# Three small waits of a matmul-bound kernel: phase ends moved to slot ends, one block's copies moved to VectorE, two more PSUM buffers for the last block

## The chip, the cores and the metric

One core of a Trainium2 chip runs the kernel. The metric is the device time in microseconds (us), as a median over runs of one execution each. The profile is one execution; its span is the time from the first to the last instruction, about 1.75 us less than the device time of the same run. TensorE is "PE" in the profile (its weight loads "PEld"), VectorE "DVE", ScalarE "ACT", GpSimd "POOL", SyncE "SP".

## The reference, cut to what matters

```python
# x: (8, 4096, 192) f32; weight: (8, 7): a causal convolution over 7 positions, one set of taps per head
w = softmax(weight, axis=-1)
y[b, s, d] = sum(w[d // 24, k] * x_padded[b, s + k, d] for k in range(7))
# moe_w_in: (192, 2048), moe_w_out: (2048, 192)
h = y.reshape(32768, 192) @ moe_w_in
out = (0.5 * h * (1 + erf(h / sqrt(2)))) @ moe_w_out     # exact GELU
```

## The kernel before

The 32768 tokens are worked on as two halves side by side: the two row halves of TensorE take one token half each. Each half is cut into 35 blocks: six of 256 tokens (0 to 5) and 29 of 512 (6 to 34). A block passes four engines:

- VectorE transposes x and does the convolution (`xT`, `acc`, `xc`). Blocks 0 and 1 are convolved on TensorE.
- TensorE multiplies with `win` into one of two PSUM buffers `hp` (each two banks). This is one *slot*; a block has 8 or 16.
- ScalarE takes the GELU of `hp` into `gT`. Slot u needs the buffer that GELU u - 2 has left.
- TensorE multiplies `gT` with `wout` into the four banks `ob`. This work is cut into *units*, and a share of the units of block n - 1 is issued behind the inner matmuls of each slot of block n.

The two groups of a 256-token block (128 tokens of each half) have two *phases* of 16 units each. In the second the row halves swap banks, and the program makes it wait for the first (`S_PH`; 0.29 us of load idle in the kernel before where nothing lies between them). The four groups of the last block are done after everything else.

```python
share = {1: [4, 8, 8, 8, 9, 9, 9, 9]}          # units of block 0 in the slots of block 1; blocks 2 to 5: 8 each

def mm2(m, g, ph, i):                          # one unit: two matmuls
    bb = banks(m, g)
    if i == 0:
        if ph == 0:
            wait_banks(t, m, g)
        else:
            t.wait_ge(S_PH, PHC[m] + g + 1)    # the first phase has ended
    if g == 0 and ph == 0:
        c = NCH[m]                             # units that one GELU serves: 2, or 1 in a 512-token block
        if i % max(c, 8) == 0:                 # GELUs of the next eight units
            last = min(NF, i + max(c, 8))
            t.wait_ge(S_GELU, SL0[m] + last // c)
    ...

def wait_banks(t, m, g):
    ...
    else:                                      # the last block
        e = k - G0[M1]                         # its group
        t.wait_ge(S_EV, EVC[M1] + (-2 if e == 0 else e - 1))   # group 1: all transposes of block 33
        if e >= 2:
            t.wait_ge(S_EVB, e - 1)

def evac(e, m, g):                             # blocks 0 to 5, on ScalarE
    ...
    e.activation(out=dst, in_=src, func=AF.Copy).then_inc(S_EVA)

m = NB - 1                                     # the last block's units
for g2 in range(0, NG[m], 2):
    for ph in range(2):
        for g in range(2):
            for i in range(NF):
                mm2(m, g2 + g, ph, i)
```

The first matmul of a block waits for VectorE's convolution of that block (`S_CV`) and for the GELU two slots back. VectorE's work on block 2 begins when x of block 2 has landed (at 19.65 us in the trace of the kernel before). SyncE issues the loads in the order x of blocks 0 and 1, the four quarters of `w_out`, x of block 2.

## Time and profile before

| | before |
|---|---|
| time, median of the 3 runs known at first | 683.61 us (683.43 to 683.99) |
| span of the profiled run | 681.6 us |
| PE busy | 675.0 us, 99% |
| DVE busy | 561.0 us, 82% |
| ACT busy | 537.3 us, 79% |

The order of reading is: busy shares on the page, busy time by stage, then the timeline at the few places where PE isn't full. PE's busy time can hold a wait (in the prediction's lines the 16 matmuls at 21.02 show 1.06 us against 0.82 for the next 16, with 0.29 us of load idle among them), so the *starts* of a slot's first weight load are the better ruler: each loss shows as a step. The prediction shows the lines.

### The profile page before, as it was taken

What the parts mean: (1) busy time and instruction counts of PE and PEld (TensorE: products, weight loads), DVE (VectorE), ACT (ScalarE), POOL (GpSimd) and SP (SyncE); (2) the same over time, 40 slices, a digit from 0 to 9 for tenths busy, and PEclk for the clock granted to TensorE, in tenths of its full rate; (3) what the DMA queues carried; (4) which work ended last, traced back from release to release, by engine and by line L of the source; (5) the groups of instructions that cost most, each with busy time, mean ns of one, the idle gap of its engine ahead of it and who ended that gap; (6) DMA issues with size and microseconds to landing.
All of it is one profiled execution on the core that took longest, in us unless ns stands there. A gap on an engine that the chain in (4) does not pass through costs nothing.

```text
span 681.6 us, 27317 instructions
## 1 busy us (share of the span) xinstructions
PE 675.0 (99%) x12576; PEld 410.1 (60%) x12576; DVE 561.0 (82%) x904; ACT 537.3 (79%) x550; POOL 38.9 (6%) x57
## 2 busy tenths in 40 slices
PE   8999999999999999999999999999999999999998
PEld 4899655555555555555555555555555555555556
DVE  6899979888889888899888898888898888988611
ACT  6899988787787777787777788777878777878772
POOL 5026000000000000000000000000000000000000
PEclk9999999999999999999999999999999999999999
DMA  9446323234332244332244422334322434310123
GB/s 222 86 101 134 79 60 75 43 75 95 96 94 58 45 91 94 95 86 47 60 94 95 94 69 46 78 94 96 94 52 46 95 94 96 83 42 21 48 49 94
DMA packets 132994, 54.79 MB, mean 80 GB/s; under 512 B 126480, under 2 KB 132752, under 8 KB 132880
## 3 DMA queue, kind: packets, MB, share of 16 engines
q1 hardware_dynamic: 130960, 51.50, 32.5%
q8 instruction: 98, 1.61, 1.0%
q0 software_dynamic: 1248, 0.79, 0.9%
q10 hardware_dynamic: 672, 0.76, 0.4%
q14 instruction: 16, 0.13, 0.1%
HBM read 28.66 MB, written 25.17 MB: 79 GB/s over the span
## 4 chain that ended last, share of the span: by engine, by line
PE 96%; ACT 2%; DMA 1%; issue 0%; DVE 0%; SPq 0%; ACTq 0%
PE hp L760 48%; PE ob L824 43%; PE ob L791 6%; ACT gT L681 2%; DMA xin<-in_x_dram 1%; PE ob L711 0%; ACT xc L191 0%; ACT osb L269 0%; DVE osb L311 0%; DVE xT L526 0%; ACT xTb L630 0%; SPq L872 0%; DVE osb L280 0%; SPq L329 0%; ACTq L629 0%
## 5 line engine op out<-in xcount | busy, mean ns | idle before, releaser
L681 ACT ACTIVATE gT<-hp 128x1024 bf16<-128x1024 f32 x512 | 523.3, 1024 | 128.8 <-PE hp L760 125.5
L760 PE MATMUL hp<-xc,win 64*64 64x512 bf16 (+2 forms) x6048 | 419.5, 366 | 1.5 <-ACT gT L681 0.7
L824 PE MATMUL ob<-gT,wout 64*64 64x512 bf16 x5376 | 366.3, 376 | 0.0
L559 DVE SCALAR_TENSOR_TENSOR acc<-xT,wcol,acc 128x512 f32<-128x512 f32 (+1 forms) x495 | 314.1, 698 | 0.0
L760 PEld LDWEIGHTS hp<-xc,win 64*64 64x64 bf16 (+1 forms) x6048 | 189.9, 106 | 134.8 <-ACT gT L681 2.5
L824 PEld LDWEIGHTS ob<-gT,wout 64*64 64x64 bf16 x5376 | 172.3, 118 | 122.8
L311 DVE STREAM_TRANSPOSE osb<-ob 128x512 f32<-128x512 f32 x84 | 74.1, 885 | 100.8 <-PE ob L824 100.8
L526 DVE STREAM_TRANSPOSE xT<-xin 128x512 f32<-128x512 f32 (+1 forms) x105 | 78.6, 797 | 3.8 <-DMA xin<-in_x_dram 3.8
L559 DVE SCALAR_TENSOR_TENSOR xc<-xT,wcol,acc 128x512 bf16<-128x512 f32 (+1 forms) x99 | 65.0, 708 | 0.0
L447 POOL COPY xT<-xT 128x18 f32<-128x18 f32 x30 | 27.9, 930 | 505.2 <-DVE xT L526 482.9
L791 PE MATMUL ob<-wout,gT 64*128 64x192 bf16 x1024 | 52.9, 243 | 0.3
L791 PEld LDWEIGHTS ob<-wout,gT 64*128 64x128 bf16 x1024 | 44.9, 94 | 5.2 <-PE ob L791 0.6
L552 DVE TENSOR_SCALAR acc<-xT,wcol 128x512 f32<-128x512 f32 (+1 forms) x90 | 37.5, 474 | 1.1
L282 ACT ACTIVATE osb<-ob 128x192 f32<-128x192 f32 x4 | 1.3, 332 | 9.5 <-PE ob L791 9.5
L280 DVE COPY osb<-ob 128x192 f32<-128x192 f32 x4 | 1.4, 358 | 8.4 <-PE ob L791 8.4
L695 PE MATMUL hp<-warm 128*128 128x512 bf16 x16 | 5.1, 485 | 1.3 <-DVE warm L463 1.3
L269 ACT ACTIVATE osb<-ob 128x384 f32<-128x384 f32 x12 | 5.8, 486 | 0.0
L654 ACT ACTIVATE acc<-xT,wcol 128x256 f32<-128x256 f32 (+1 forms) x9 | 5.2, 575 | 0.0
L695 PEld LDWEIGHTS hp<-warm 128*128 128x128 bf16 x16 | 1.8, 119 | 4.0 <-issue 1.9
L384 POOL DMA_DIRECT2D win<-in_moe_w_in_dram x6 | 3.9, 658 | 0.8 <-POOLq L905 0.8
L711 PE MATMUL ob<-xTb,dg 64*64 64x256 bf16 (+1 forms) x112 | 3.2, 245 | 0.7 <-ACT xTb L630 0.7
L193 DVE CAST xc<-ob 64x256 bf16<-64x256 f32 (+3 forms) x8 | 2.8, 357 | 1.3 <-PE ob L711 1.1
(31 smaller groups left out, 22.4 us busy)
## 6 DMA issues: line engine op xcount, KB each, us to landing
out_dram<-osb SPq DMA_DIRECT2D x122, 192.0 KB, 3.1
xin<-in_x_dram SPq DMA_DIRECT2D x116, 192.0 KB, 4.1
xin<-in_x_dram SPq DMA_DIRECT2D x20, 96.0 KB, 4.2
woutf<-in_moe_w_out_dram SPq DMA_DIRECT2D x4, 384.0 KB, 6.2
win<-in_moe_w_in_dram POOLq DMA_DIRECT2D x4, 96.0 KB, 4.6
win<-in_moe_w_in_dram POOLq DMA_DIRECT2D x2, 192.0 KB, 5.1
out_dram<-osb SPq DMA_DIRECT2D x8, 48.0 KB, 1.9
out_dram<-osb ACTq DMA_DIRECT2D x4, 96.0 KB, 1.9
```

The lines of the kernel that those rows point to most:

```text
L269: e.activation(out=dst, in_=src, func=AF.Copy).then_inc(S_EVA)
L311: v.transpose(ap(osb[m % 2], j, [[8 * C, 128], [C // 2, TB // 32], [NP, 32]]), bank(ring(m, j)),).then_inc(S_EV)
L447: g.tensor_copy(dst, src).then_inc(S_HALO)
L526: v.transpose(ap(xT[n % 2], p * XW + HX, [[NP * XW, 128], [1, w]]), ap(xin[n % NX], p, [[TB // 32 * DQ, 128], [D if n == 0 else DQ, w // 3 ...
L552: ins = v.tensor_scalar(a, src, wk, None, ALU.mult)
L559: ins = v.scalar_tensor_tensor(dst, src, wk, a, op0=ALU.mult, op1=ALU.add)
L654: a.activation(out=acc[n % 2][:, p * TB : p * TB + w], in_=ap(xT[n % 2], p * XW + HX, [[NP * XW, 128], [1, w]]), func=AF.Copy, scale=wcol[ ...
L681: a.activation(out=ap(gT[n % 2], i * c * 2 * w, dst), in_=ap(hp[u % 2], 0, src), func=AF.Gelu,).then_inc(S_GELU)
L695: t.matmul(hp[1][:, 0:512], warm[:, 0:128], warm[:, :])
L760: ins = t.matmul(hp[u % 2][fo : fo + fw, o : o + w], ap(win, f1, [[NP * F, 64], [2, fw]]), xc[n % 2][r, p * TB : p * TB + w], start=(p == ...
L791: ins = t.matmul(bank(bb[sub], w=C), gT[m % 2][r, c0 : c0 + 128], wout[r, CH[sub][i] * C : (CH[sub][i] + 1) * C], start=(ph == 0 and i == ...
L824: ins = t.matmul(bank(ring(m, j), slice(64 * h, 64 * h + 64), w), ap(wout, 64 * hf * NF * C + CH[h][i] * C + j, [[NF * C, 64], [NP, 64]],) ...
```

## The change

It removes three waits. Block 0's phases are to end with a slot, so that inner matmuls lie between a phase and its partner. Block 5's two copies out of PSUM go from ScalarE to VectorE. The last block's groups 1 and 3 write `hp`, free by then, and its first phase waits for four GELUs at a time.

```diff
-    NA = 6
+    NA = 5                    # ScalarE copies blocks 0 to 4
-    M0, M1 = NA, NB - 1
+    M0, M1 = 6, NB - 1
 ... # banks(): the last block's odd groups
+            if g % 2:
+                return [hp[g // 2][:, h * TB : h * TB + C] for h in range(2)]
 ... # wait_banks()
+            elif g % 2:
+                t.wait_ge(S_GELU, SL0[NB] - 1 + g // 2)
             else:
-                e = k - G0[M1]
-                t.wait_ge(S_EV, EVC[M1] + (-2 if e == 0 else e - 1))
-                if e >= 2:
-                    t.wait_ge(S_EVB, e - 1)
+                t.wait_ge(S_EV, EVC[M1] - 2 + g)
 ... # evac()
-            e.activation(out=dst, in_=src, func=AF.Copy).then_inc(S_EVA)
+            if m < NA:
+                e.activation(out=dst, in_=src, func=AF.Copy).then_inc(S_EVA)
+            else:
+                e.tensor_copy(dst, src).then_inc(S_EV)
 ... # VectorE's list
-            side = []
+            side = [((M0 + 2, 7 * g), evac, v, M0 - 1, g) for g in range(NG[M0 - 1])]
 ... # mm2()
-                    if i % max(c, 8) == 0:
-                        last = min(NF, i + max(c, 8))
-                        t.wait_ge(S_GELU, SL0[m] + last // c)
+                    if i % 4 == 0:
+                        t.wait_ge(S_GELU, SL0[m] + (i + 4) // c)
-            share = {1: [4, 8, 8, 8, 9, 9, 9, 9]}
+            share = {1: [4, 12, 8, 8, 8, 8, 8, 8]}
 ... # mm2_t(): block 6 waits for VectorE's copies in place of ScalarE's
```

More of the change, by code (lines that the diff above doesn't have):

```diff
@@ L87, in bass_lightweight_conv__then__act_gelu_exact_kernel @@
     CH = [[(8 * hf + i) % NF for i in range(NF)] for hf in range(2)]
-    assert all(WS[n] == TB for n in range(M0, NB))
+    assert all(WS[n] == TB for n in range(M0, NB)) and NG[NB - 1] == 4 and SL0[NB] % 2 == 0
     OUTS = []
@@ L237, in banks @@
             if m < M0:
-                return (0, 1) if (G0[m] + g) % 2 == 0 else (2, 3)
+                return [bank(2 * ((G0[m] + g) % 2) + h, w=C) for h in range(2)]
+            if g % 2:
+                return [hp[g // 2][:, h * TB : h * TB + C] for h in range(2)]
             r = NP * (M1 - 1 - M0)
-            e = (G0[m] - G0[M1] + g) % 2
-            return sorted((b % 4 for b in ((r + 3, r), (r + 1, r + 2))[e]))
+            return [bank(b, w=C) for b in sorted((b % 4 for b in ((r + 3, r), (r + 1, r + 2))[g // 2]))]
         def wait_ev(e, m, g):
@@ L265, in evac @@
                 e.wait_ge(S_OUT[m % 2], OUTS[m - 2])
-            b0, b1 = banks(m, g)
             dst = ap(osb[m % 2], g * C, [[8 * C, 128], [4 * C, 2], [1, C]])
-            src = ap(ob, 512 * b0, [[2048, 128], [512 * (b1 - b0), 2], [1, C]])
-            e.activation(out=dst, in_=src, func=AF.Copy).then_inc(S_EVA)
+            src = ap(ob, 1024 * ((G0[m] + g) % 2), [[2048, 128], [512, 2], [1, C]])
+            if m < NA:
+                e.activation(out=dst, in_=src, func=AF.Copy).then_inc(S_EVA)
+            else:
+                e.tensor_copy(dst, src).then_inc(S_EV)
         def evac_half(e, g, h):
@@ L277, in evac_half @@
             dst = osb[m % 2][:, (4 * h + g) * C : (4 * h + g + 1) * C]
-            src = bank(banks(m, g)[h], w=C)
+            src = banks(m, g)[h]
             if h == 0:
@@ L791, in mm2 @@
                     ins = t.matmul(
-                        bank(bb[sub], w=C),
+                        bb[sub],
                         gT[m % 2][r, c0 : c0 + 128],
@@ L809, in mm2_t @@
                     if ps < 2:
-                        if m == M0:
-                            t.wait_ge(S_EVA, G0[M0] - 1 + ps)
-                        else:
-                            t.wait_ge(S_EV, EVC[m] - 2 + ps)
+                        t.wait_ge(S_EV, EVC[m] - (1 if m == M0 else 2) + ps)
                     if ps > 0:
```

## The prediction

Passages of the record are cut, with the cuts marked: a paragraph of rules that no trace of this case shows; the lag by which the author explained the gap at 29.14 us (by the table below the load comes 0.12 us after VectorE's end in that trace); and the estimate of VectorE's copies with two sentences that rest on it, because its rate was taken from no trace. The margin of 2.7 us in rival 2 is the author's estimate.

> **What bounds the kernel now.** I began with the page. Its first part gives TensorE 675.0 of 681.6 us busy, VectorE 82%, ScalarE 79%; its chain of work that ended last is 96% PE. So TensorE's own stream is the bound and only about 6.6 us of the span hold no matmul. A busy PE can still be stretched, so I next asked for the busy time by stage. I put the borders at the first block's output matmuls, at block 2, at block 6 (the first of 512 columns), at block 7 and at the last block's output matmuls. The columns are the window, its length, and busy us with the number of instructions of each engine:
>
> ```profile
> core 0: us, PE busy (x) PEld busy (x) DVE busy (x) ACT busy (x) POOL busy (x), PEclk, DMA share, GB/s
> 19.04:29.18 10.14, 10.01 (x209) 8.91 (x206) 9.50 (x25) 8.04 (x9) 0.47 (x3) 1.00 0.34 64
> 29.18:71.26 42.08, 42.08 (x898) 42.05 (x898) 42.05 (x90) 38.09 (x50) 16.59 (x4) 1.00 0.46 107
> 71.26:87.32 16.06, 15.93 (x230) 9.94 (x226) 15.99 (x26) 16.06 (x19) 0.53 (x2) 1.00 0.34 76
> 87.32:667.60 580.28, 580.28 (x10754) 329.47 (x10752) 478.69 (x727) 459.17 (x450) 10.61 (x26) 1.00 0.32 73
> 667.60:681.60 14.00, 11.02 (x260) 10.41 (x256) 3.00 (x6) 2.05 (x5) 0.00 (x0) 1.00 0.42 115
> ```
>
> The 580 us from block 7 to the last block are PE from end to end, and the change touches no instruction there. All that it can win lies in three short places: block 1's slots, block 6, and the tail. In two windows ScalarE or VectorE is as full as PE: 16.06 of 16.06 us ScalarE in block 6, and VectorE 9.50 of 10.14 us just before block 2. There a wait can pass from one engine to another. So I read the three places in the timeline (start, length, engine, line, operation, count, and in brackets the idle time before and what ended it).
>
> Place 1, block 0's output matmuls (L791) inside block 1's slots, up to block 2's first matmuls (L760 at 29.14):
>
> ```profile
> 21.02 1.06 PE L791 MATMUL ob<-wout,gT 64*128 64x192 bf16 x16
> 21.57 0.28 PEld L791 LDWEIGHTS ob<-wout,gT 64*128 64x128 bf16 x8 [0.29 <-PE ob L791]
> 22.57 0.82 PE L791 MATMUL ob<-wout,gT 64*128 64x192 bf16 x16
> 27.07 0.53 PEld L791 LDWEIGHTS ob<-wout,gT 64*128 64x128 bf16 x14 [0.29 <-PE ob L791]
> 27.77 1.26 DVE L559 SCALAR_TENSOR_TENSOR xc<-xT,wcol,acc 128x256 bf16<-128x256 f32 x3
> 29.14 0.58 PEld L760 LDWEIGHTS hp<-xc,win 64*128 64x128 bf16 x12 [0.15 <-issue]
> ```
>
> The reader is to see two stalls in the middle of a run of output matmuls, and that VectorE's last three results for block 2 end at 27.77 + 1.26 = 29.03, just before block 2's first weight load.
>
> Place 2, block 6, where ScalarE is gapless:
>
> ```profile
> 79.89 0.49 ACT L269 ACTIVATE osb<-ob 128x384 f32<-128x384 f32 x1
> 80.26 7.86 ACT L681 ACTIVATE gT<-hp 128x1024 bf16<-128x1024 f32 x8
> 80.06 0.83 PE L760 MATMUL hp<-xc,win 64*128 64x512 bf16 x6
> 81.35 0.82 PE L760 MATMUL hp<-xc,win 64*128 64x512 bf16 x6
> 82.34 0.81 PE L760 MATMUL hp<-xc,win 64*128 64x512 bf16 x6
> ```
>
> Slots start every 0.98 us, but the one after the copy comes 81.35 - 80.06 = 1.29 us later.
>
> Place 3, the tail, weight loads of the last block's first two output phases and the transposes that empty PSUM:
>
> ```profile
> 667.60 0.61 PEld L791 LDWEIGHTS ob<-wout,gT 64*128 64x128 bf16 x16 [0.40 <-issue]
> 667.73 1.56 DVE L311 STREAM_TRANSPOSE osb<-ob 128x512 f32<-128x512 f32 x2 [6.44 <-PE ob L824]
> 668.37 0.61 PEld L791 LDWEIGHTS ob<-wout,gT 64*128 64x128 bf16 x16 [0.16 <-ACT gT L681]
> 669.34 9.19 PEld L791 LDWEIGHTS ob<-wout,gT 64*128 64x128 bf16 x224 [0.37 <-DVE osb L311]
> ```
>
> Two waits, then 224 loads without one.
>
> [...]
>
> **The change part by part.**
>
> *Block 0's phases.* Block 0 has 64 output units (two matmuls each) in block 1's eight slots. The shares 4, 8, 8, 8, 9, 9, 9, 9 add up to 4, 12, 20, 28, 37, 46, 55, 64. The swap within a group comes at units 16 and 48, in the middle of slots 2 and 6, so it stalls. The new shares 4, 12, 8, ... add up to 4, 16, 24, 32, 40, 48, ...: both swaps fall behind a slot's 12 inner matmuls (0.66 us), longer than the stall. What the stalls cost: the slot at 21.02 lasts until 21.91, 0.89 us for 16 matmuls where the next takes 0.66, so 0.23. The one at 26.68 lasts until 27.66, 0.98 against 0.74 for 18, so 0.24. Together PE reaches block 2 about 0.47 us sooner, at some 28.5 in place of 28.98 us for the first load.
>
> But block 2's first matmul also needs VectorE's convolution of block 2. That run begins at 19.65 us, when a transfer of x lands, and goes without a gap to 29.03. Nothing in it waits for block 1's matmuls, and no instruction of it is changed. PE already arrives some 0.15 us too early; the page calls that gap "issue"[...]. So I expect the whole 0.47 us to become a longer wait at 29.1 and this part to bring **0**.
>
> *Block 5's copies.* Two ScalarE copies of 486 ns (at 79.89 and 88.02) go to VectorE. In block 6 ScalarE's GELUs (L681) run back to back, and a slot's matmuls can start only when the GELU two slots earlier is done. The copy at 79.89 therefore goes straight to PE: 81.35 - 80.06 = 1.29 less the usual 0.98 is **0.31 us** saved. The second copy, at block 7's start, cost PE nothing: slots in block 7 take 1.295 us and ScalarE is idle 0.27 us in each. [...] They stand at operations 0 and 7 of block 8's list, at about 84.7 and 89.5 us. The results they read are complete at about 79 and 87 us, so VectorE doesn't wait. PE needs the first bank pair at 88.0 and the second at 94, so PE doesn't wait. [...]
>
> *The tail.* The finer waits on the GELUs (four units at a time, no longer eight) let units 8 to 11 start before the last GELU ends at 668.32; units 12 on start at 668.6, after it. Loads go at 0.66 us per 16 units, so 667.60 + 0.66 = 668.26 against 668.37: 0.11 saved. The second group's phase now writes the inner layer's first PSUM buffer, free since the last GELU but one, and no longer waits for the two transposes: 668.37 + 0.66 = 669.03 against 669.34, 0.31. Together **0.42 us**. The copy and store behind the last matmul stay as they are.
>
> Sum: 0 + 0.31 + 0.42 = 0.73 us; 683.61 - 0.73 = 682.88.
>
> **The rivals.**
> 1. *The phases' 0.47 us is kept*, because the gap at 29.14 was only "issue". For it: the profile names no VectorE wait there. Against: the ends match within 0.1 us. It would make 682.4.
> 2. *VectorE becomes late.* For it: VectorE is 99% busy in block 6 (15.99 of 16.06), and two copies are added. Against: it works a block ahead, and its margin before PE needs the first bank pair is about 2.7 us. If the copies came late, PE would stand at block 7's start for up to a microsecond: 683.2 to 684.
> 3. *ScalarE stays the limit of block 6.* Its GELUs go at 0.98 us each, the same as PE's slots, so there is no slack to catch up. That halves nothing, but if the copy's loss was partly recovered later the part is 0.2, not 0.31: 683.0.
> 4. *The tail's gain is lost behind the last store*, if an earlier store delays the last. Against: stores of one slice (96 KB) land in about 2 us and come 1.3 us or more apart, in the same order as before. It would make 683.3.
>
> **Range and chances.** The runs of before span 683.43 to 683.99, so a median of three moves by some 0.2 us alone; rivals 1 and 4 give the borders: 682.4 to 683.5. For over 2% the time would have to change by 13.7 us. All matmul-free time is 6.6 us, so faster by that is out of reach, and a new wait of that size has no place in the two slots that VectorE fills. Chances: faster 0.005, same 0.99, slower 0.005.
>
> **What would show it.** In the changed profile the load idle of 0.29 us should be gone from block 1, and block 2's first load should still start at about 29.1 us, after an idle of about 0.6. If it starts at 28.6, rival 1 holds. Block 6's slots should be even at 0.98 us, and block 7 start 0.31 us sooner. [...] The last block's 256 loads should run without a wait on VectorE or ScalarE, from start to end in 10.5 us where they took 10.93. The prediction is wrong if PE waits for VectorE at block 7, or if the total is under 682.4 or above 683.5.

## The result, and the profile after

| | before | after |
|---|---|---|
| median of 6 runs | 683.48 us (683.28 to 683.99) | 682.98 us (682.34 to 683.50) |
| ratio | | 0.9991, 95% interval 0.9978 to 1.0004 |
| span of the profiled run | 681.6 us | 680.6 us |

A ratio is the mean time of one kernel's runs over that of the other's of the same rounds, so not quite the ratio of the medians. Executions over 1.5% slower than the fastest of the same kernel are left out of the means. The interval reaches from 1.5 us faster to 0.3 us slower, so the times alone don't show the gain; the traces do. The busy time by stage of the changed kernel, with the borders at the same instructions as before:

```profile
core 0: us, PE busy (x) PEld busy (x) DVE busy (x) ACT busy (x) POOL busy (x), PEclk, DMA share, GB/s
19.34:28.87 9.53, 9.53 (x208) 9.03 (x206) 9.49 (x25) 7.75 (x9) 0.32 (x1) 1.00 0.26 52
70.95:86.68 15.73, 15.73 (x228) 9.35 (x224) 15.70 (x26) 15.73 (x18) 0.45 (x1) 1.00 0.35 78
666.97:680.56 13.59, 10.74 (x260) 10.51 (x256) 3.02 (x6) 2.04 (x5) 0.00 (x0) 1.00 0.43 117
```

Block 1's slots took 9.53 us (10.14 before), block 6 15.73 (16.06), the tail 13.59 (14.00). The first window is the surprise: I had expected it to end where it had ended. Here is its timeline in the changed kernel, behind the line of the kernel before that belongs beside the first:

```profile
19.65 1.35 DVE L526 STREAM_TRANSPOSE xT<-xin 128x256 f32<-128x256 f32 x3 [1.54 <-DMA xin<-in_x_dram]
```

```profile
19.24 1.35 DVE L529 STREAM_TRANSPOSE xT<-xin 128x256 f32<-128x256 f32 x3 [0.77 <-DMA xin<-in_x_dram]
21.53 0.70 PEld L793 LDWEIGHTS ob<-wout,gT 64*128 64x128 bf16 x16
26.79 0.70 PEld L793 LDWEIGHTS ob<-wout,gT 64*128 64x128 bf16 x16
27.35 1.27 DVE L562 SCALAR_TENSOR_TENSOR xc<-xT,wcol,acc 128x256 bf16<-128x256 f32 x3
27.47 0.62 PEld L763 LDWEIGHTS hp<-xc,win 64*128 64x128 bf16 x12
28.79 0.62 PEld L763 LDWEIGHTS hp<-xc,win 64*128 64x128 bf16 x12
```

The loads at 21.53 and 26.79 are the first behind the two phase swaps, and the idle time of 0.29 us is gone from both: a swap that cost 0.23 to 0.24 us before costs nothing behind the 12 inner matmuls (0.66 us) of a slot; both slots' steps are 1.31 us, like their neighbours' 1.31 to 1.32. VectorE ended block 2 at 28.62 us, 0.41 earlier than before, because x of block 2 had landed 0.41 earlier. TensorE loads for block 2 at 28.79, 1.32 us after its last slot's load, its usual step: it did not wait. The margin was small: VectorE's end plus the 0.12 us that TensorE follows it by where it waits (see the experiments) is 28.74, only 0.05 us sooner. The timeline of block 6, ScalarE, TensorE and VectorE:

```profile
71.80 16.80 ACT L684 ACTIVATE gT<-hp 128x1024 bf16<-128x1024 f32 x17
79.75 0.81 PE L763 MATMUL hp<-xc,win 64*128 64x512 bf16 x6
80.72 0.81 PE L763 MATMUL hp<-xc,win 64*128 64x512 bf16 x6
84.40 0.55 DVE L272 COPY osb<-ob 128x384 f32<-128x384 f32 x1
89.14 0.55 DVE L272 COPY osb<-ob 128x384 f32<-128x384 f32 x1
100.31 0.89 DVE L314 STREAM_TRANSPOSE osb<-ob 128x512 f32<-128x512 f32 x1 [3.34 <-PE ob L823]
```

Seventeen GELUs run without a break, the slots go on at 0.98 us, and VectorE still has 3.34 us to spare. The tail:

```profile
666.97 1.27 PEld L793 LDWEIGHTS ob<-wout,gT 64*128 64x128 bf16 x32 [0.40 <-issue]
667.09 1.58 DVE L314 STREAM_TRANSPOSE osb<-ob 128x512 f32<-128x512 f32 x2 [6.45 <-PE ob L823]
668.22 1.33 PEld L793 LDWEIGHTS hp<-wout,gT 64*128 64x128 bf16 x32
```

The second group's loads start while the transposes that used to hold them (until 668.67) still run.

### The profile page after: what moved, and what is told of

Read it like the earlier page. It is cut to its first block, busy times and chain, and to the rows that moved or that the text cites. A ratio compares the mean times of both kernels' runs of the same rounds, so it can differ in the third digit from the quotient of the medians.

```text
span 680.6 us, 27316 instructions
## 1 busy us (share of the span) xinstructions
PE 674.6 (99%) x12576; PEld 407.5 (60%) x12576; DVE 561.7 (83%) x906; ACT 536.5 (79%) x548; POOL 38.9 (6%) x57
## 4 chain that ended last, share of the span: by engine, by line
PE 98%; ACT 1%; DMA 1%; DVE 0%; SPq 0%; issue 0%; ACTq 0%
PE hp L763 48%; PE ob L823 43%; PE ob L793 5%; PE hp L793 1%; DMA xin<-in_x_dram 1%; ACT gT L684 1%; PE ob L714 0%; ACT xc L191 0%; DVE xT L529 0%; ACT xTb L633 0%; SPq L871 0%; DVE osb L283 0%; SPq L332 0%; ACTq L632 0%
## 5 line engine op out<-in xcount | busy, mean ns | idle before, releaser
L763 PEld LDWEIGHTS hp<-xc,win 64*64 64x64 bf16 (+1 forms) x6048 | 187.6, 106 | 136.1 <-ACT gT L684 2.6
L793 PE MATMUL ob<-wout,gT 64*128 64x192 bf16 x896 | 46.8, 243 | 0.0
L793 PEld LDWEIGHTS ob<-wout,gT 64*128 64x128 bf16 x896 | 38.6, 94 | 5.2 <-issue 0.4
L793 PE MATMUL hp<-wout,gT 64*128 64x192 bf16 x128 | 5.9, 243 | 0.0
L793 PEld LDWEIGHTS hp<-wout,gT 64*128 64x128 bf16 x128 | 5.3, 94 | 0.0
```

What stands on the lines that cost most here:

```text
L763: ins = t.matmul(hp[u % 2][fo : fo + fw, o : o + w], ap(win, f1, [[NP * F, 64], [2, fw]]), xc[n % 2][r, p * TB : p * TB + w], start=(p == ...
L793: ins = t.matmul(bb[sub], gT[m % 2][r, c0 : c0 + 128], wout[r, CH[sub][i] * C : (CH[sub][i] + 1) * C], start=(ph == 0 and i == 0), stop=(p ...
```

## The experiments

My theory after the result: *the start of block 2 is the later of two arrivals.* TensorE arrives at the earliest 10.45 us after block 1's first load with the new shares, 10.93 with the old (later where block 1's second slot waits for a GELU, 0.36 us in one trace, or for `w_out`, 0.37 us in another). VectorE arrives when x of block 2 has landed, plus 9.4 us of work. Each arrival hangs on a transfer of the first 20 us, which scatters from run to run (x of block 2 was ready between 19.2 and 21.1 us in six traces); what follows block 2's start is fixed to 0.04 us. The rival for the phases is that the short gap before block 2 was only issue overhead, so that their 0.47 us is always gained. The rivals for the other parts are those of the prediction.

The table has the profiled run of each kernel, in us, from the starts and ends of instructions in its trace. "Block 1" is from block 1's first weight load to block 2's; "behind DVE" is from the end of VectorE's last result for block 2 to that load; "block 6" is from block 6's first load to block 7's; "tail" is from load 0 to load 240 of the last 256; "rest" is the span less the start of block 2. The buffers alone and the two late kernels were run once each, for their traces; their single times say nothing.

| kernel | block 2 starts | block 1 | behind DVE | block 6 | tail | rest |
|---|---|---|---|---|---|---|
| before | 29.14 | 11.14 | 0.12 | 16.13 | 10.26 | 652.47 |
| after | 28.79 | 10.45 | 0.16 | 15.81 | 9.83 | 651.77 |
| phases alone | 30.17 | 10.58 | 0.12 | 16.13 | 10.25 | 652.48 |
| block 5 alone | 29.09 | 10.94 | 0.14 | 15.81 | 10.26 | 652.19 |
| tail alone | 30.04 | 10.93 | 0.60 | 16.12 | 9.83 | 652.08 |
| tail, buffers only | 30.63 | 11.62 | 0.12 | 16.14 | 9.94 | 652.16 |
| before, VectorE late | 30.70 | 12.02 | 0.12 | 16.13 | 10.26 | 652.46 |
| after, VectorE late | 29.82 | 11.77 | 0.12 | 15.83 | 9.83 | 651.73 |
| after, a tap on ScalarE | 30.28 | 11.45 | 0.12 | 15.83 | 9.83 | 651.74 |
| after, x of block 2 earlier | 29.48 | 10.77 | 0.70 | 15.81 | 9.83 | 651.76 |
| the same, other order of units | 30.05 | 11.91 | 0.62 | 15.81 | 9.83 | 651.77 |

### The phases alone

```diff
-            share = {1: [4, 8, 8, 8, 9, 9, 9, 9]}
+            share = {1: [4, 12, 8, 8, 8, 8, 8, 8]}
```

> The kernel before with the new shares of block 0's results alone. Theory (block 2's start is the later of TensorE's arrival and VectorE's end of block 2's convolution, and the latter hangs on when x of block 2 lands): from block 1's first weight load to block 2's first, 10.45 us where TensorE arrives last (11.14 before), and longer, up to 11.1, where VectorE ends last; the load idle of 0.29 us at the phase swaps is gone either way. Block 6 stays at 16.13 us from its first load to block 7's, the last 256 loads at 10.26 us from load 0 to load 240. Time: 0 to 0.5 us under before. Rival (the swaps cost nothing on the path): block 2 starts exactly as far behind block 1 as before, 11.1 us.

The load idle at the swaps is gone, and block 1 took 10.58 us: between the two values, because in this run VectorE ended last by a little (0.12 behind DVE). With the old shares TensorE would have come at 19.59 (block 1's first load here) + 10.93 = 30.52 at the earliest, so 0.35 us or more of the 0.47 was gained in this run.

```profile
28.79 1.27 DVE L559 SCALAR_TENSOR_TENSOR xc<-xT,wcol,acc 128x256 bf16<-128x256 f32 x3
30.17 0.58 PEld L760 LDWEIGHTS hp<-xc,win 64*128 64x128 bf16 x12
```

The times say nothing: 683.76 us against 683.81, ratio 0.9997 (0.9983 to 1.0010).

### Block 5's copies alone

```diff
-    NA = 6
+    NA = 5                    # with evac(), side and mm2_t() as in the change
```

> The kernel before with block 5's two copies on VectorE alone. Theory: block 6 from its first load to block 7's first takes 15.81 us (16.13 before), ScalarE's GELUs there run 16 or more in one gapless group, VectorE's copies take 0.55 us each and its idle time before the first transpose of block 6's results shrinks by about 1.2 us; block 1 as before (10.97 or more), tail 10.26. Time 0.3 us under before. Rival (VectorE becomes late): a wait of TensorE at block 7's start, and no gain.

As the theory has it: block 6 took 15.81, with 17 GELUs in one group, and VectorE's idle time before its first transpose fell from 4.57 to 3.3 us. No wait at block 7. The time, 683.81 us with a ratio of 0.9996 (0.9984 to 1.0009), resolves nothing.

### The tail alone, and its two halves

```diff
 # the changed kernel with the old shares and with block 5 on ScalarE
-    NA = 5
+    NA = 6
-            share = {1: [4, 12, 8, 8, 8, 8, 8, 8]}
+            share = {1: [4, 8, 8, 8, 9, 9, 9, 9]}
```

> The kernel before with the tail's part alone: two PSUM buffers more for the last block, and waits for four GELUs at a time. Theory: the last 256 loads take 9.83 us from load 0 to load 240 (10.26 before), without a wait on ScalarE or VectorE; block 6 16.13, block 1 as before. Time 0.42 us under before. Rival (the gain goes lost behind the last store): the loads are faster but the span from the last matmul to the end grows by as much.

The tail took 9.83 us, and from load 240 to the end of the span 3.76 us as before (3.75), so nothing is lost behind the last store. The time was 683.59 us, ratio 0.9995 (0.9983 to 1.0008), unresolved again. With the old waits for eight GELUs put back:

```diff
-                    if i % 4 == 0:
-                        t.wait_ge(S_GELU, SL0[m] + (i + 4) // c)
+                    if i % max(c, 8) == 0:
+                        last = min(NF, i + max(c, 8))
+                        t.wait_ge(S_GELU, SL0[m] + last // c)
```

> As the tail's part alone, but with the old waits for eight GELUs at a time. Theory: the wait on ScalarE before load 16 stays (0.77 us from load 0 to 16, as before), the wait on VectorE before load 32 is gone (0.66 or less in place of 0.98); load 0 to load 240 takes 9.94 us, 0.1 more than with the finer waits.

The weight loads of that kernel's tail:

```profile
669.86 0.61 PEld L794 LDWEIGHTS ob<-wout,gT 64*128 64x128 bf16 x16 [0.16 <-ACT gT L684]
670.46 1.33 PEld L794 LDWEIGHTS hp<-wout,gT 64*128 64x128 bf16 x32
```

The wait on ScalarE is back, that on VectorE is not: 9.94 us. The buffers are worth 0.31 us and the finer waits 0.11.

### VectorE made late, in both kernels

```diff
+                    if (b, o) == (2, NP):
+                        v.memset(dly[:, :], 0.0)      # 128 x 1024 f32, behind block 2's transposes
```

> The kernel before with a memset of 1024 elements on VectorE (about 1.1 us, estimated from the 256 elements that took 0.27) after block 2's transposes, to make VectorE late for certain. Theory: block 2's first load comes about 0.1 us after VectorE's last result of block 2, whatever TensorE did; from the start of block 2's transposes on VectorE to that load 10.6 us (9.5 before). Rival (TensorE's arrival sets it): block 2's first load does not move.

> The changed kernel with the same memset. Theory: from the start of block 2's transposes to block 2's first load 10.6 us, the same as in the kernel before with the memset, so the phases' 0.47 us is worth nothing there and TensorE waits about 1.0 us or more. Rival: 0.4 to 0.5 us less than with the memset in the kernel before.

The kernel before and the changed one, VectorE's last results of block 2 and TensorE's first loads:

```profile
29.31 1.27 DVE L560 SCALAR_TENSOR_TENSOR xc<-xT,wcol,acc 128x256 bf16<-128x256 f32 x3
30.70 0.58 PEld L763 LDWEIGHTS hp<-xc,win 64*128 64x128 bf16 x12 [0.66 <-ACT gT L684]
```

```profile
28.43 1.27 DVE L563 SCALAR_TENSOR_TENSOR xc<-xT,wcol,acc 128x256 bf16<-128x256 f32 x3
29.82 0.58 PEld L766 LDWEIGHTS hp<-xc,win 64*128 64x128 bf16 x12 [1.30 <-ACT gT L687]
```

From the start of block 2's transposes (20.36 and 19.49) to that load it took 10.34 and 10.33 us, the same in both kernels. I had said 10.6: the memset cost 0.8 us, not 1.1. The changed kernel's TensorE arrived sooner and waited longer, 1.30 us against 0.66, and gained nothing. So VectorE's end does set block 2's start when it comes last, and the phases are then worth 0. Note the releaser in the brackets: the load waits for two semaphores, and the profile names ScalarE. The load comes 0.12 us after VectorE's end in both kernels, however long the wait, and so it does in every trace of the table where VectorE came last.

### VectorE made shorter

```diff
+    # block 2's first tap of its third part on ScalarE, in block 1's third slot
+                        a.activation(out=acc[0][...], in_=ap(xT[0], ...), func=AF.Copy,
+                                     scale=wcol[:, KS - 1 : KS]).then_inc(S_K2)
```

(A tap is one of the convolution's seven positions: one multiply, then six multiply-adds.)

> The changed kernel with one of block 2's first taps on ScalarE (idle there), which shortens VectorE's run for block 2 by one operation of 0.29 us. Theory: from the start of block 2's transposes to VectorE's last result 9.1 us (9.4 before and after), so TensorE's arrival sets block 2's start more often, and block 1 takes 10.45 us from first load to block 2's first. Time: 0 to 0.3 us under the changed kernel, around 682.7. If the tap on ScalarE delays a GELU that TensorE needs, block 1 is longer than 10.45 us and the gain is lost.

VectorE's run was 9.12 us, as expected, but in the profiled run x of block 2 landed only at 21.02, so VectorE came last all the same (block 1 took 11.45 us, not 10.45), and `w_out` came late too (0.37 us of load idle in the second slot). The time was 683.78 us (682.55 to 684.00), ratio to the kernel before 0.9990 (0.9976 to 1.0004): no different from the change. The landing's scatter, 1.9 us in six other traces, is larger than the 0.29 us removed.

### x of block 2 before the last quarter of w_out

```diff
             for i in range(4):
+                if i == 3:
+                    load(sp, 2)
                 g = WG[i]
 ...
-            load(sp, 2)
-            share = {1: [4, 12, 8, 8, 8, 8, 8, 8]}
+            share = {1: [4, 0, 12, 8, 8, 8, 8, 16]}
```

> The changed kernel with x of block 2 fetched before the last quarter of w_out, and block 1's second slot left without output matmuls, as that quarter comes later. Theory: x of block 2 lands about 1.5 us earlier (at 17.5 to 18.2), VectorE's last result of block 2 about 1 us earlier (27.6 to 28.1), and no wait of TensorE on VectorE is left at block 2. TensorE may lose some tenths to the later w_out. Time 682.5 to 683.2: at or under the changed kernel if the landing was what limited it, above it if the later w_out costs more.

x of block 2 landed at 18.80, not before 18.2, and the last quarter of `w_out` at 20.35 (17.40 in the changed kernel). TensorE no longer waited for VectorE (0.70 us behind it), but lost 0.32 us in block 1, because it waited 0.41 us for a GELU behind the empty slot:

```profile
20.20 1.44 DVE L555 TENSOR_SCALAR acc<-xT,wcol 128x256 f32<-128x256 f32 x3
20.41 0.84 POOL L460 CAST wout<-woutf 128x768 bf16<-128x768 f32 x1 [3.06 <-DMA woutf<-in_moe_w_out_dram]
20.66 0.55 PEld L763 LDWEIGHTS hp<-xc,win 64*128 64x128 bf16 x12 [0.41 <-ACT gT L684]
21.30 0.96 PEld L793 LDWEIGHTS ob<-wout,gT 64*128 64x128 bf16 x24
```

The cast of the last quarter ended at 21.25, just in time: no wait is seen before the loads at 21.30. VectorE ended at 28.77, not at 27.6 to 28.1: its run took 9.95 us in place of 9.39, because the three `tensor_scalar` took 1.44 us in place of 0.88 beside that cast. (In the next order of units they took 1.45 us, again beside the cast; why was not tried.) The time was 683.00 us (682.97 to 683.21 in five runs), ratio to the kernel before 0.9986 (0.9973 to 0.9998), the only interval here below 1. The scatter of five runs was 0.24 us, where the nine runs of the kernel before beside it spread over 1.7 us (but the next kernel, with the same order of loads, spread over 0.60). It was not timed beside the changed kernel, whose ratios to before are much the same, so I don't call it better.

### The changed kernel again, and another order of units

> The changed kernel again, for a second profile and beside the next run. Theory: whatever the time when block 2 starts (its first weight load, the later of TensorE's arrival at 10.45 us after block 1's first load and VectorE's last result plus 0.115 us), the rest is fixed: from that load to the span's end 651.7 to 651.8 us (652.4 to 652.5 in the kernel before). Rival (the scatter of the time arises anywhere in the kernel): the rest differs by more than 0.1 us. Time 682.3 to 683.6.

The profile (the first of its five runs, 697.42 us):

```profile
core 0: 695.7 us, clock 0.970
```

So its "rest" can't be compared; that test rests on the four variants of the changed kernel in the table. Its four fast runs took 682.47 to 683.51 us; ratio 0.9988 (0.9975 to 1.0002).

```diff
 # as x earlier; block 0's units: four of group 0, four of group 1, then the rest
-            share = {1: [4, 0, 12, 8, 8, 8, 8, 16]}
+            share = {1: [4, 4, 12, 12, 8, 8, 8, 8]}
+                        [(g, 0, i) for g in range(2) for i in range(4)]
+                        + [(g, 0, i) for g in range(2) for i in range(4, NF)]
+                        + [(g, 1, i) for g in range(2) for i in range(NF)]
```

(GpSimd's halo is its copy of the last positions of the block before; its edit is left out above.)

> The changed kernel with x of block 2 before the last quarter of w_out, GpSimd's halo of block 2 before its cast of that quarter, and block 0's output units in an order in which the second group's first four stand in block 1's second slot, so that TensorE has work while the last quarter comes. Theory: VectorE's last result of block 2 comes 9.4 us after the start of its transposes, well before TensorE arrives; block 1 takes 10.4 to 10.6 us; the rest 651.7 to 651.8; the time 682.3 to 682.9 with a scatter of some 0.3 us, under the changed kernel. Rival[...]: TensorE waits for w_out in the third slot, block 1 takes 10.8 us or more, and the time is that of the changed kernel.

A miss; what the rival foretold of block 1 came. TensorE, VectorE and GpSimd in block 1:

```profile
22.22 0.94 PEld L795 LDWEIGHTS ob<-wout,gT 64*128 64x128 bf16 x24 [1.56 <-POOL wout L462]
20.86 1.45 DVE L557 TENSOR_SCALAR acc<-xT,wcol 128x256 f32<-128x256 f32 x3
21.16 1.00 POOL L462 CAST wout<-woutf 128x768 bf16<-128x768 f32 x1 [2.68 <-DMA woutf<-in_moe_w_out_dram]
```

The last quarter of `w_out` landed at 21.11 and TensorE stood still for it (1.56 us of load idle, until the cast had ended). Block 1 took 11.91 us, the time was 683.58 us, ratio to before 0.9997 (0.9984 to 1.0011). The changed kernel's four fast runs beside it had a median of 682.80, so `w_out` cost more than x gained: x of block 2 landed at 19.46 in this trace, no earlier than in the changed kernel (19.21). Why the landings came so was not tested.

## Why the prediction was right or wrong, point by point

The time was right: 682.98 us, where I had said 682.88 with 682.4 to 683.5. That is a weak test: the interval of the ratio holds a gain of 0 as well as one of 1.2 us, so the nearness of the two numbers is partly luck, and the parts have to be judged by the traces.

- **Block 5's copies, 0.31 us: right.** Block 6 went from 16.13 to 15.81, in the change and alone. VectorE's copies took 0.55 us each (0.49 on ScalarE) and left it 3.34 us idle, and rival 2 (VectorE late) and rival 3 (a part of the loss recovered) fell. (That the change touches no instruction from block 7 on, as the prediction says first, isn't so: one of the two copies moved lies there, at 88.02 us, as it says itself further on.)
- **The tail, 0.42 us: right,** in the sum and in its halves (0.11 and 0.31). Rival 4 fell. The prediction has a slip here that did no harm: the 0.66 us are for 16 loads, which are eight units, not 16.
- **The phases, 0: wrong as a fixed number.** The stalls' cost of 0.47 us was right (10.93 against 10.45 where TensorE arrives last). The failing step was "So I expect the whole 0.47 us to become a longer wait at 29.1". It took the landing of x of block 2 in one profile as if it were the same in every run. That wait is what happens if VectorE comes last, as the late runs show, and in the profiled run of the change it did not, so block 2 started at 28.79 us without a wait, and not at 29.1 after one of 0.6. Rival 1 was wrong in its reason: the gap before block 2 was a wait on VectorE.
- **What the phases are worth instead:** from 0 to 0.47 us by the run. An estimate from the traces with the transfers untouched (before, after, and the four of single parts): with TensorE's arrival at block 1's first load plus 10.93 or 10.45, and VectorE's at its end plus 0.12, the difference of the two maxima is 0, 0.48, 0.35, 0.02, 0.48 and 0, on average 0.22 us. In these six traces what counts is less how late x of block 2 lands than how long after x of block 1: TensorE's first load of block 1 follows the start of VectorE's transposes of block 1 by 5.56 to 5.60 us in five of the six traces (5.92 in block 5 alone). The transposes of block 2 begin 7.24, 6.47, 6.65, 7.33, 6.52 and 7.69 us behind those of block 1, and the phases bring nothing, or 0.02, in the three traces where this is over 7.

The rest behind block 2 fell from 652.47 to 651.77 us, 0.70: 0.32 of block 6 and 0.42 of the tail, less 0.04 between blocks 2 and 6. That stretch took 42.08 us in the traces where TensorE came last and 42.03 to 42.06 where VectorE did, as in the kernel before. (Why was not shown.) With an average of 0.22 us for the phases, 0.9 us would be my estimate of the whole; the two measured ratios, 0.9991 and 0.9988, are 0.6 and 0.8 us, each with about 0.9 us of uncertainty either way.

What stays open: why the landings scatter. In the six traces above x of block 2 was ready for VectorE between 19.2 and 21.1 us, a scatter of 1.9 us, and the four of single parts, all taken on one chip, span 19.6 to 21.1 by themselves, so it is not only a difference between chips. No experiment here took the transfers apart.

## What to carry to other kernels

Where a stage starts at the later of two arrivals, a saving on one of them is worth a share that hangs on the scatter of the other; before predicting 0 or all of it, ask what each arrival hangs on and whether that thing, above all a transfer in the start (here the page shows the DMA engines 90% busy or more in the first 17 us, about 40% in the next), is the same in every run. When the gain is smaller than the scatter of the time, measure in the trace from one regular instruction to another: here the steps showed to 0.01 us in single profiles, while five timed runs couldn't tell 0.4 us from nothing. Behind the last place where an outside event can intrude, the whole remaining run may be a constant (here 652.46 to 652.48 us in the kernel before, with the new shares and with VectorE late, and 651.73 to 651.77 us in the changed kernel and its variants), and a change is best judged on that constant.
